# Relu² attention, Fourier mixing and a feed-forward block on one core: the last four token groups' first products taken jointly in two pairs, two first groups of 384 tokens, add and relu fused, and single events of the order model delayed or claimed

## The chip, the cores and the metric

One core of a Trainium2 chip runs the whole program. The metric is the device time of one execution in microseconds (us); for the kernel before, three runs gave 577.59, 578.49 and 578.52 us, median 578.49. Beside the times there is one profiled execution of it. Engines are named as the profile names them: PE multiplies matrices, PEld loads its weights, DVE, ACT and POOL work elementwise, SP issues most of the transfers. PSUM is the memory into which PE accumulates, SBUF the one that holds everything else on the core.

## What is computed

Eight batches, twelve heads, 448 positions, head size 64; the twelve heads side by side give rows of 768. The feed-forward block widens 768 to 3072 and back.

```python
scores = scale * np.matmul(q, k.transpose(0, 1, 3, 2))
attn = np.maximum(scores, 0.0) ** 2 / S
x = np.matmul(attn, v)                      # heads side by side: (8, 448, 768)
mixed = np.real(np.fft.fft(np.fft.fft(x, axis=1), axis=2))
u = x + mixed
un = (u - mean(u)) / np.sqrt(var(u) + 1e-06)
out = u + np.maximum(un @ w_ch1, 0.0) @ w_ch2
```

## The kernel before, in words

**Stages.** For each batch the program makes scores on PE (`score`), takes relu on ACT and the square on DVE or ACT (`squares`, `square`), multiplies by v (`attention`), folds the result and multiplies it by tables of cosines and sines (`fold`, `halves`, `mix`, `mix_rows`), adds x, normalises the rows (`rows` inside `mix_rows`), and stores u and the normalised un in DRAM (`u_store`, `n_store`). `turns` reads un back transposed, by transposing transfers that SP issues, into the tiles `unT`. The 3584 rows of all batches are then cut into token groups by the list `GT`, and `ffn` multiplies one group after another by the two weights. Groups do not end where batches do.

**Groups.** Before, `GT` gives groups of 384, 512 and 384 tokens and then nine of 256, numbered 0 to 11. A group's first product is 24 column blocks of w_ch1, each six matmuls with as many columns as the group has tokens (L1793); relu takes the sums out of PSUM into `hT`. The second product goes by blocks of 128 tokens. A block can be taken alone (`WHOLES`, `whole`), with 4 times 12 matmuls of 384 columns, or two blocks can be taken as a pair (`PAIRS`, class `Pair`), with 7 times 12 (L1933). The pair gets by with seven products in place of eight, as fast 2x2 block multiplication does, by using sums of blocks of `hT` (`Pair.early`, `Pair.late` on DVE) and sums of blocks of w_ch2 (`weight_sums`). What a product adds to the output goes through `add` (L1515) on DVE to a tile `o`, which holds rows of u and is then stored by SP (`outputs`).

**The last two groups.** Groups 10 and 11 take also the first product in that way (`last_two`): for each of twelve steps i, `main`, `second` and `third` issue seven products of three matmuls with 256 columns (L1635) in place of eight. Their operands are sums of blocks of w_ch1, made in SBUF that attention has left (`quarter_sums`, L1549, 24 sums of 768 columns), and four sums `Tk` of the two groups' `unT` (L1586). Partial sums are copied from PSUM by ACT (`copy`, L1644); DVE adds such a copy to another PSUM tile (`sum_out`, L1649) and takes the relu of the result in a second instruction (L1652). A `unT` tile has two homes that groups use in turn; a home is free when the group in it has ended its first product (`BUNT`).

**What sets the order.** Nothing is ordered by hand. Each stage is a generator that says which engine it needs, for how long by a model, and after what (`need`). `Streams.run` takes at each step the stream that could start earliest by the model and, between equals, the one of the lower rank, and emits it, so the order on every engine is fixed when the program is built. On the chip semaphores keep it correct, and an engine waits where the model was too hopeful. Attention on the later batches is let in between feed-forward matmuls by the rule `lead`: a piece of attention waits until `progress` (feed-forward work done, in batches) has come within `LEAD` of it.

## Time and profile before

| | us |
|---|---|
| three runs, median (lowest, highest) | 578.49 (577.59, 578.52) |
| span of the profiled execution, first to last instruction | 576.0 |
| median of the runs less that span | 2.5 |
| PE busy in it | 565.0 |
| DVE, ACT, POOL busy in it | 446.9, 336.9, 134.0 |

The page has no time of its own for the profiled execution beside its span; what lies around a span (launch and end) is taken as the 2.5 us by which the median of the runs exceeds it. Busy times are unions of an engine's instructions. A matmul's own duration in the profile runs from its start to its modelled end and overlaps with the next one's, so a rate is read from a run of many matmuls (length over count), not from the mean of one. Stretches are given in us from the span's start.

### The profile page before, as it was taken

How to read it: one execution, taken by the hardware profiler on the slowest of the kernel's cores; microseconds unless marked ns; L12 is line 12 of the kernel's file. 1: busy time of each engine (PE TensorE's matmuls, PEld its weight loads, DVE VectorE, ACT ScalarE, POOL GpSimd, SP SyncE). 2: the span in 40 equal slices, each digit the busy share in tenths (PEclk: the TensorE clock that was granted, in tenths of full speed). 3: DMA queues.
4: the chain of work that ended last, by engine and by line, in shares of the span. 5: the costliest groups of instructions: out<-in, count | busy, mean ns of one | idle time of the engine just before them, and what ended most of it. 6: DMA issues, size and time to landing. Idle time of an engine off the chain costs nothing.

```text
span 576.0 us, 11341 instructions
## 1 busy us (share of the span) xinstructions
PE 565.0 (98%) x4339; PEld 358.5 (62%) x4344; DVE 446.9 (78%) x1030; ACT 336.9 (59%) x538; POOL 134.0 (23%) x187
## 2 busy tenths in 40 slices
PE   8999999999999999999999999999999999999997
PEld 6466556544465546556757567568567786868864
DVE  6988775986688877997798879978978994267872
ACT  5977772977745676667559658856573160406400
POOL 8527102410134113321333116112220230000000
PEclk9999999999999999999999999999999999999999
DMA  9999999656938985799769977996654342223012
GB/s 125 206 211 249 202 219 181 174 109 78 202 78 223 175 140 119 161 167 193 140 136 197 201 126 161 177 173 113 141 107 94 109 142 85 66 73 93 2 41 97
DMA packets 133505, 81.84 MB, mean 142 GB/s; under 512 B 77516, under 2 KB 128716, under 8 KB 133452
## 3 DMA queue, kind: packets, MB, share of 16 engines
q0 software_dynamic: 40320, 33.63, 37.2%
q1 hardware_dynamic: 93132, 47.50, 36.6%
q8 instruction: 34, 0.56, 0.4%
q14 instruction: 19, 0.16, 0.1%
HBM read 62.91 MB, written 26.25 MB: 155 GB/s over the span
## 4 chain that ended last, share of the span: by engine, by line
PE 87%; DVE 9%; ACT 3%; issue 1%; DVEq 0%; ACTq 0%
PE psF L1793 31%; PE psF L1933 21%; PE psS L857 6%; PE psF L785 5%; PE psF L1821 4%; PE psS L1933 4%; PE psS L1635 3%; PE psF L1848 3%; PE psS L1332 2%; DVE sq L887 2%; ACT sq L870 1%; PE psS L785 1%; PE psS L2011 1%; PE psF L1635 1%; PE psS L932 1%; PE psS L1307 1%
## 5 line engine op out<-in xcount | busy, mean ns | idle before, releaser
L1793 PE MATMUL psF<-unT,w 128*128 128x256 bf16 (+2 forms) x1435 | 197.6, 294 | 1.3 <-ACT hT L1780 0.7
L870 ACT ACTIVATE sq<-psS 112x896 bf16<-112x896 f32 x192 | 165.2, 930 | 39.6 <-PE psS L857 39.2
L1793 PEld LDWEIGHTS <-w 128*128 128x128 bf16 x1440 | 137.5, 98 | 58.7 <-issue 12.9
L887 DVE TENSOR_TENSOR sq<-sq 112x896 bf16<-112x896 bf16 x163 | 98.4, 620 | 15.9 <-ACT sq L870 14.9
L1780 ACT ACTIVATE hT<-psF 128x512 bf16<-128x512 f32 (+3 forms) x144 | 71.7, 513 | 66.5 <-PE psF L1793 65.3
L1933 PEld LDWEIGHTS <-hT 128*128 128x128 bf16 x720 | 69.0, 98 | 50.3 <-issue 5.9
L1933 PE MATMUL psF<-w,hT 128*128 128x384 bf16 x378 | 67.1, 326 | 0.7 <-DVE xT L612 0.7
L1515 DVE TENSOR_TENSOR o<-psF,o 128x384 f32<-128x384 f32 x80 | 44.2, 553 | 25.2 <-PE psF L1933 20.8
L857 PE MATMUL psS<-qkT 64*128 64x448 bf16 (+1 forms) x384 | 52.8, 358 | 2.5 <-ACT sq L870 1.9
L413 POOL DMA_DIRECT2D vn<-in_v_dram x24 | 17.5, 730 | 105.4 <-PE psS L857 86.0
L1176 POOL TENSOR_TENSOR u<-tp,xn 112x385 f32<-112x385 f32 (+2 forms) x14 | 13.6, 974 | 109.0 <-DVE tp L1158 81.8
L857 PEld LDWEIGHTS <-qkT 64*128 64x128 bf16 (+1 forms) x384 | 17.3, 101 | 31.1 <-issue 24.1
L612 DVE TENSOR_SCALAR xT<-psF 128x224 bf16<-128x224 f32 x54 | 18.5, 383 | 21.8 <-PE psF L785 21.7
L785 PE MATMUL psF<-sq,vn 112*64 112x448 bf16 x264 | 31.3, 358 | 0.9 <-DVE hT L1778 0.9
L1204 ACT ACTIVATE un<-u,nmr,rstd 113x768 bf16<-113x768 f32 (+2 forms) x23 | 23.0, 1022 | 14.9 <-DVE nmr L1191 14.6
L413 POOL DMA_DIRECT2D qn<-in_q_dram x21 | 15.2, 724 | 62.7 <-DVE qkr L509 53.0
L1933 PE MATMUL psF<-wsum,hT 128*128 128x384 bf16 x162 | 28.8, 326 | 0.0
L1185 DVE BATCH_NORM_STATS2 stats<-u 112x6 f32<-112x384 f32 (+2 forms) x56 | 28.8, 540 | 0.0
L785 PEld LDWEIGHTS <-vn 112*64 112x64 bf16 x336 | 15.8, 109 | 19.6 <-issue 13.4
L884 ACT ACTIVATE sq<-sq 112x896 bf16<-112x896 bf16 x29 | 27.3, 950 | 0.5
L1821 PE MATMUL psF<-w,hT 128*128 128x384 bf16 x144 | 24.9, 326 | 0.0
L1848 PE MATMUL psF<-w,hT 128*128 128x384 bf16 x144 | 24.4, 326 | 0.0
(228 smaller groups left out, 783.2 us busy)
## 6 DMA issues: line engine op xcount, KB each, us to landing
out_dram<-o SPq DMA_DIRECT2D x56, 192.0 KB, 2.3
vn<-in_v_dram POOLq DMA_DIRECT2D x24, 224.0 KB, 5.0
qn<-in_q_dram POOLq DMA_DIRECT2D x21, 224.0 KB, 4.5
kn<-in_k_dram POOLq DMA_DIRECT2D x21, 224.0 KB, 7.3
w<-in_moe_w_ch_dram POOLq DMA_DIRECT2D x12, 384.0 KB, 13.2
w<-in_moe_w_ch_dram POOLq DMA_DIRECT2D x4, 1152.0 KB, 15.5
utop<-u SPq DMA_DIRECT2D x12, 336.0 KB, 3.8
o<-utop SPq DMA_DIRECT2D x16, 192.0 KB, 4.2
```

Of the source, the lines that this page charges most:

```text
L413: nc.gpsimd.dma_start(out=t, in_=src[b, hs].rearrange("h (p j) d -> p h (j d)", j=4))
L785: nc.tensor.matmul(av[h * Dh:(h + 1) * Dh, 0:S], lhsT=vn[:, c, h0 + h, :], rhs=sq[:, h, :], start=(c == 0), stop=(c == 3))
L857: nc.tensor.matmul(sc[:wide, h, 0:S].rearrange("k (c q) -> k c q", c=4), lhsT=flat[ps, k0:k0 + wide], rhs=qT[ps, m % 2], start=True, stop= ...
L870: nc.scalar.activation(r, sc[:R, :, 0:S], AF.Relu)
L887: nc.vector.tensor_tensor(r, r, r, op=ALU.mult)
L1185: nc.vector.bn_stats(stats[:n, hf, :], u[:n, hf * (D // 2):(hf + 1) * (D // 2)])
L1515: nc.vector.tensor_tensor(o, pc[:, 0:DH], o, op=ALU.add)
L1780: nc.scalar.activation(hs, ps, AF.Relu)
L1793: nc.tensor.matmul(ph[:, i * N:(i + 1) * N], lhsT=w1_sb[m][hf][:, (jj + i) * 128:(jj + i + 1) * 128], rhs=unT[:, m, 0:N], start=(m == 0), ...
L1821: nc.tensor.matmul(pc[:, 0:DH], lhsT=block(j, c), rhs=w2(j, hf), start=(j == 0), stop=(j == JC - 1))
L1848: nc.tensor.matmul(pc[:, 0:DH], lhsT=block(2 * i + k, c), rhs=weights[i], start=(start and i == 0), stop=(i == KP - 1), skip_group_check=True)
L1933: nc.tensor.matmul(pc[:, 0:DH], lhsT=lhs[i], rhs=rhs[i], start=(start and i == 0), stop=(i == KP - 1), skip_group_check=True)
```

## The change

Seven things change.

1. `GT` becomes 384, 384 and then eleven groups of 256; there are 13 groups, 0 to 12. `WHOLES` becomes `[[0, 1, 2], [2]]` and all groups but the first have one pair.
2. `last_two` becomes `joint(number)`, and runs twice: groups 9 and 10, then groups 11 and 12 (`JOINTS`). The buffers that the two share are taken once (`spread`), the four `Tk` are made once for each, and the `unT` homes of groups 9 and 10 are free when all 36 ends of their first products have been issued (`through`). The second group's block sums get tiles of their own (`ownsum`).
3. `sum_out` issues one instruction, `TENSOR_ADD_SAT` with the limits 0 and the largest float, for the add and the relu.
4. Of batch 1 the 128 rows of the second tile no longer are turned on PE; they go to DRAM by a new `part_store` (one scattering store by POOL, one row by SP) and come back by `turns`.
5. `HEAD` and `NUDGE` shift the model's start time of some kinds of events, or of single ones, when streams are compared; the start that is booked afterwards is the unshifted one.
6. The model's turned q and k count as ready 1.1055 us later (`TURNED`), stored rows 1.0 us later (`STORED`); `LEAD` is 2.7 less a slope of 0.1 for each batch still to come.
7. The fourth weight sum is made once and not partly twice; `Banks.take` may choose a PSUM bank by which tile its neighbour is in (`apart`).

```diff
@@ -57,9 +62,24 @@
+HEAD = {
+    ('attentions', 'PE', 2): -0.6, ('attentions', 'PE', 3): -0.619, ('chain_b', 'PE', 2): 0.232,
...
+}
+NUDGE = {
+    ('attentions.1', 45): 0.8, ('attentions.1', 48): 0.28, ('chain_a.1', 4): 0.28, ('chain_a.1', 8): 0.8,
...
+}
@@ -112,7 +138,7 @@
-                key = (ok is not None and not ok(), max(t), s[1][eng != "PE"])
+                key = (ok is not None and not ok(), max(t) + HEAD.get((s[3], eng, phase), 0.0) + NUDGE.get((s[4], s[5]), 0.0), s[1][eng != "PE"])
@@ -194,12 +222,13 @@
-    GT = [0, 384, 896] + list(range(1280, B * S + 1, 256))
+    GT = [0, 384] + list(range(768, B * S + 1, 256))
...
+    JOINTS = list(range(9, NGR, 2))
@@ -521,9 +551,9 @@
-                    c.t = e
+                    c.t = e + TURNED
@@ -749,7 +779,8 @@
-            lead = b + ((p if n else pa) - (0 if left is None else 4)) / NB - LEAD
+            lead = b + ((p if n else pa) - (0 if left is None else 4)) / NB
+            lead -= LEAD - SLOPE * (B - lead)
@@ -1259,6 +1291,19 @@
+    def part_store(ch, t):
+
+        un = lambda: uns[1][2 * ch + 1]
+        if ch:
+            e = yield need("SP", 0.1, [t])
+            nc.sync.dma_start(out=nbot[1][HS - 128:HS - 127, :], in_=un()[0:1])
+            n_stored[1][3].t = sch.dma(e, D * 2)
+            return
+        e = yield need("POOL", 1.1, [t])
+        nc.gpsimd.indirect_dma_start(out=nbot[1], out_offset=bass.IndirectOffsetOnAxis(ap=back[0], axis=0),
+                                     in_=un(), in_offset=None)
+        n_stored[1][1].t = sch.dma(e, 128 * D * 2) + 1.0
@@ -1379,7 +1430,7 @@
-    WHOLES = [[0, 1, 2], [2, 3], [2]] + [[]] * (NGR - 3)
+    WHOLES = [[0, 1, 2], [2]] + [[]] * (NGR - 2)
     PAIRS = [[], [0]] + [[0]] * (NGR - 2)
@@ -1498,10 +1550,11 @@
-        for b in range(NGR - 2):
+        for b in range(JOINTS[0]):
             yield need("SP", 0.0, [group_ready[b]])
             yield from ffn(b)
-        yield from last_two()
+        for n in range(len(JOINTS)):
+            yield from joint(n)
@@ -1577,20 +1636,20 @@
+        for c, g in enumerate(JOINTS):
+            yield need("DVE", 0.0, [group_ready[g], group_ready[g + 1]])
+            b1, b2 = groups[g][2], groups[g + 1][2]
...
@@ -1635,7 +1704,13 @@
+        def through(e):
+            to_go[0] -= 1
+            if not to_go[0]:
+                BUNT.free += [e, e]
@@ -1646,10 +1721,8 @@
             e = yield need("DVE", dve(N), deps, [BH[t]] if hta is not None else [])
-            nc.vector.tensor_tensor(dst, q[:, 0:N], u, op=ALU.add)
+            nc.vector._custom_dve(TENSOR_ADD_SAT, out=dst, in0=q[:, 0:N], in1=u, s0=FMAX, s1=0.0)
             done(e)
-            e = yield need("DVE", 0.2)
-            nc.vector.tensor_scalar(dst, dst, 0.0, None, op0=ALU.max)
             return e + LATENCY["DVE"] + SLACK
```

How the change moves instructions is shown at three places, with the numbers of the tiles. The first is DVE at the start of the joint stage; `hT` and `hB` are the relu'd first products of the two groups, `copies` the partial sums that ACT copied, `psS` and `psF` tiles of PSUM. Before:

```order
L1649 TENSOR_TENSOR hT_968<-psS_7062,copies_7065 128x256
L1652 TENSOR_SCALAR hT_968<-hT_968 128x256
L1649 TENSOR_TENSOR hT_968<-psS_7063,copies_7066 128x256
L1652 TENSOR_SCALAR hT_968<-hT_968 128x256
L1649 TENSOR_TENSOR hT_968<-psS_7064,copies_7067 128x256
```

And now:

```order
L1724 ISA hT_968<-psS_6621,copies_6624 128x256
L1724 ISA hT_968<-psS_6622,copies_6625 128x256
L1724 ISA hT_968<-psS_6623,copies_6626 128x256
L1724 ISA hT_968<-psF_6651,copies_6629 128x256
L1724 ISA hB_6513<-psS_6621,copies_6624 128x256
L1724 ISA hB_6513<-psS_6622,copies_6625 128x256
```

Each add with its relu has become one instruction, 36 for each joint, and no relu stands behind it on DVE.

The second place is SP's queue ahead of the program's last two groups: the transposing transfers that bring their `unT` from the stored rows (`ntop` and `nbot` with a batch's number), and what each waits for. Before (the transposes for group 11 stand twelve rows below those for group 10 that are shown):

```order
L1239 DMA ntop7_93<-un_6621 112x768 [waits DMAHW1_49,Activation_49]
L1280 DMA_TRANSPOSE unT_3354<-nbot6_100 128x6x64 [waits PE_49]
L1280 DMA_TRANSPOSE unT_3354<-ntop7_93 128x6x192 [waits DMAHW3_49,DMAHW1_49]
L1496 DMA out_0_dram<-o_6542 128x384 [waits DMAHW4_49,DVE_49]
L1496 DMA out_0_dram<-o_6559 128x384 [waits DMAHW5_49,DVE_49]
L1496 DMA out_0_dram<-o_6557 128x384 [waits DMAHW6_49,DVE_49]
```

And now, in front of groups 11 and 12:

```order
L1544 DMA o_6703<-ubot5_82 128x384 [waits DMAHW4_49]
L1324 DMA_TRANSPOSE unT_2455<-nbot6_100 128x6x64 [waits PE_49]
L1324 DMA_TRANSPOSE unT_2455<-ntop7_93 128x6x192 [waits DMAHW0_49]
L1324 DMA_TRANSPOSE unT_2455<-ntop7_93 128x6x32 [waits DMAHW1_49,PE_49]
L1548 DMA out_0_dram<-o_6632 128x384 [waits DMAHW2_49,DVE_49]
L1324 DMA_TRANSPOSE unT_2455<-nbot7_101 128x6x224 [waits DMAHW3_49,DMASW4_49]
```

The transposes of both groups now stand together behind a wait for PE, with the store of the output tile `o_6632` between them, which waits for DVE. On DVE the second and last add to that tile stands here, behind the sums of the first joint's pair (`s2` is a sum of blocks of `hT`):

```order
L1996 TENSOR_TENSOR hT_968<-hT_968,s2_2224 128x6x128
L1996 TENSOR_TENSOR hT_968<-hT_968 128x4x128
L1996 TENSOR_TENSOR hT_968<-hT_968 128x2x128
L1568 TENSOR_TENSOR o_6632<-psS_6622,o_6632 128x384
L1984 TENSOR_TENSOR quarter_6474<-hB_6516 128x256
```

So group 12 is asked for once that add is done.

The third place is DVE around the last batch's mixing (its `CAST pc`), where the sums of w_ch1 blocks (`quarter`) begin; `tp`, `qs` and `u` belong to the batch's rows. Before:

```order
L1515 TENSOR_TENSOR o_6128<-psF_6315,o_6128 128x384
L1158 TENSOR_TENSOR tp_6351<-psS_6332,qs_6348 113x385
L1160 TENSOR_TENSOR qs_6348<-psS_6332,qs_6348 113x385
L1549 TENSOR_TENSOR quarter_6306<-w1_4_0_502,quarter_6305 128x768
L1515 TENSOR_TENSOR o_6128<-psF_6217,o_6128 128x384
L1176 TENSOR_TENSOR u_6375<-qs_6348,xn_5833 113x385
L1178 TENSOR_TENSOR u_6375<-tp_6351,xn_5833 113x383
```

And now:

```order
L1402 CAST pc_6175<-psS_6145 114x2x2x193
L1603 TENSOR_TENSOR quarter_6105<-quarter_6104,w1_1_0_463 128x768
L1603 TENSOR_TENSOR quarter_6106<-w1_4_0_502,quarter_6105 128x768
L1568 TENSOR_TENSOR o_5933<-psF_6162,o_5933 128x384
L1603 TENSOR_TENSOR quarter_6107<-w1_2_0_483,w1_5_0_516 128x768
L1189 TENSOR_TENSOR tp_6198<-psS_6179,qs_6195 113x385
L1191 TENSOR_TENSOR qs_6195<-psS_6179,qs_6195 113x385
```

The sums stand among the last batch's rows as before, two more of them ahead of the rows; behind them one group's two products lie ahead of the joint stage, where there were two groups.

More of the change, by code (lines that the diff above doesn't have):

```diff
@@ L45, in __init__, with take @@
         self.make, self.ids, self.tiles = make, [(0.0, i) for i in range(n)], {}
-    def take(self):
+    def take(self, apart=None):
         first = min(self.ids)
+        if apart is not None:
+            held = {i // 2 for _, i in self.tiles.values() if i < 6}
+            first = min(self.ids, key=lambda x: (x[0] > apart, x[1] // 2 in held, x))
         self.ids.remove(first)
@@ L105, in run @@
             best = spare = None
+            now = self.engine["PE"]
+            phase = sum(now >= x for x in PHASES)
             for s in self.streams:
@@ L124, in run @@
                 best = spare
-            (_, start, _), s = best
+            s = best[1]
             eng, dur, deps, bufs, ok = s[2]
+            start = max([self.engine[eng]] + [d.t if isinstance(d, Cell) else d for d in deps]
+                        + [sorted(p.free)[bufs.count(p) - 1] for p in set(bufs)])
             for p in bufs:
@@ L1271, in turns @@
                 n = n_stored[bb]
-                deps = n[half::2]
+                yield need("SP", 0.0, n[half::2])
+                deps = [c.t + STORED for c in n[half::2]]
                 e = yield need("SP", 1.5, deps, [BUNT] if g is None else [])
-                if g is None and k == 2:
-                    g = work.tile([128, MC, 512], BF16, name="unT", tag="unT1", bufs=1)
-                elif g is None:
+                if g is None:
                     if pair_homes is None:
@@ L1286, in second_turned, with left @@
     def second_turned():
+        second_un[2].t = 0.0
         yield need("SP", 0.0, second_un)
-        e = max(c.t for c in second_un)
-        BUN[0].free.append(e)
-        un_left.t = group_ready[1].t = e
+        group_ready[1].t = max(c.t for c in second_un)
+        def left():
+            yield need("SP", 0.0, n_stored[1][1::2])
+            un_left.t = max(c.t for c in second_un + n_stored[1][1::2])
+            BUN[0].free.append(un_left.t)
+        sch.add(left(), (1, 1))
     first_pps, first_chan = [None, None], [Cell(), Cell()]
@@ L1567, in quarter_sums @@
                 yield from form(4, m, hf, w1_part(0, m + 3, hf), S_[2][m, hf], ALU.subtract)
-        ga, gb = NGR - 2, NGR - 1
+        yield need("DVE", 0.0, [], [BQ[0][1], BQ[1][1]])
+        for n, x in enumerate("qk"):
+            own[n].append((0, 8, work.tile([128, 8, 128], BF16, name="ownsum", tag=f"{x}n1", bufs=1)))
         yield need("DVE", 0.0, [un_ready[B - 1][1]], [BXN] + [BQ[2]] * 3)
@@ L1704, in third @@
             product(q, 1, 3, i, Tk[4], False, True)
+            through(e1)
             def leave(e):
@@ L1729, in last_two @@
             sch.add(p.chain_b(), (6.9 + 1 * n, 0))
-        yield need("SP", 0.0, pairs[1].done)
+        yield need("SP", 0.0, pairs[0].done + pairs[1].done)
+        for x in BH:
+            x.free.append(max(d.t for p in pairs for d in p.done))
     class Set:
```

134 lines of the change are left out of this document (77 added, 57 removed), and 5 rows, old and new, of the table NUDGE.

## The prediction

> **What bounds the kernel now.** I read the page's busy times and slices first, then busy times by stretch, then the chain of waits.
>
> ```profile
> span 576.0 us, 11341 instructions
> PE 565.0 (98%) x4339; PEld 358.5 (62%) x4344; DVE 446.9 (78%) x1030; ACT 336.9 (59%) x538; POOL 134.0 (23%) x187
> PE   8999999999999999999999999999999999999997
> DVE  6988775986688877997798879978978994267872
> PE 87%; DVE 9%; ACT 3%; issue 1%; DVEq 0%; ACTq 0%
> ```
>
> PE is full in all slices but the first and the last; DVE is the next engine. Where PE is not busy shows by stretch: 0 to 92 us (start), to 448 (attention mixed with the feed-forward block; at 448.13 the last batch is mixed), to 517 (two groups alone), to 550 (the joint first product), to the end.
>
> ```profile
> core 0: us, PE busy (x) PEld busy (x) DVE busy (x) ACT busy (x) POOL busy (x), PEclk, DMA share, GB/s
> 0.00:92.20 92.20, 86.75 (x804) 52.51 (x805) 70.82 (x168) 66.65 (x101) 40.61 (x83) 1.00 1.18 199
> ...
> 92.20:448.13 355.93, 353.94 (x2587) 213.36 (x2591) 292.81 (x647) 232.84 (x354) 84.47 (x96) 1.00 0.81 150
> 448.13:517.18 69.05, 69.05 (x533) 51.67 (x531) 44.92 (x100) 20.86 (x35) 8.90 (x8) 1.00 0.30 94
> 517.18:550.14 32.96, 32.80 (x285) 27.68 (x283) 26.80 (x85) 16.60 (x48) 0.00 (x0) 1.00 0.15 46
> 550.14:576.00 25.86, 22.43 (x139) 13.31 (x136) 11.52 (x31) 0.00 (x0) 0.00 (x0) 1.00 0.22 77
> ```
>
> PE is idle 5.45 us before 92 us, 1.99 in the long middle, 0.16 in the joint product and 3.43 at the end. The granted clock is 1.00 throughout. So the span is PE's work plus 11 us, and a change is worth what it takes from PE's work, unless something new makes PE wait.
>
> **The change, part by part.** PE's rates come from unbroken runs in the chain of waits (start, length, what, number of matmuls):
>
> ```profile
> 124.96 5.29 PE psF L1793 x24
> 136.46 3.99 PE psF L1793 x18
> 458.60 15.72 PE psF L1793 x144
> 474.32 13.66 PE psF L1933 x84
> 529.89 2.62 PE psS L1635 x24
> 570.62 1.96 PE psS L1933 x12
> 572.61 0.56 DVE o L1515
> ```
>
> A matmul of 512 columns (first two rows) costs 220 to 222 ns, one of 256 109.2 (15.72 / 144; 2.62 / 24 says the same of the joint product), one of 384 162.6 (13.66 / 84).
>
> *First products.* Counted over both programs, seven plain groups of 256 and two of 384 stay; what goes is the group of 512, 144 matmuls: 144 x 0.2204 = 31.7 us. What comes is a second joint, 12 x 7 x 3 = 252 matmuls: 252 x 0.1092 = 27.5 us. Net -4.2. Bounds: the rates of 256 and 384 lie on a line of 0.417 ns a column plus 2.4 ns, which makes 512 cost 216 ns, 31.1 us and a net of -3.6; the busy time of the 512 rows as it stands, 32.2 below, makes it -4.7.
>
> ```profile
> L1793 PE MATMUL psF<-unT,w 128*128 128x512 bf16 x139 | 32.2, 380 | 0.3
> L1108 PE MATMUL psS<-rev,un x18: 190/208/219, 48.0 to 114.1; 128*128 128x64 bf16 x6, 128*128 128x127 bf16 x6, 97*128 97x97 bf16 x6
> ```
>
> *Second products.* Six of the 28 blocks were taken alone and eleven pairs; now four and twelve. A pair has 84 matmuls, two single blocks 96: -12 x 0.1626 = -1.95.
>
> *Rows turned on PE.* Six matmuls of 127 columns go (second row above); at half of a 256-column one, 0.055 each, -0.33. In their place stand one scattering store on POOL, one row and two more transposes on SP. POOL's busiest stretch here is 40.6 of 92.2 us, and neither is on PE's path; I cost this at nothing. It would cost something if group 2 waited for those rows; group 2's first product stands behind group 1's two, which is 144 x 0.163 + 132 x 0.1626 = 45 us of cover.
>
> *Fused add and relu.* The nearest rows of DVE, the add and the relu:
>
> ```profile
> L1649 DVE TENSOR_TENSOR hT<-psS,copies 128x256 bf16<-128x256 f32 x16 | 6.7, 421 | 1.5 <-ACT copies L1644 1.3 <-PE psS L1635 0.2
> L1652 DVE TENSOR_SCALAR hT<-hT 128x256 bf16<-128x256 bf16 x24 | 5.4, 227 | 0.8
> ```
>
> The fused instruction costs at least the add, 0.42 us, and I take that, since it reads and writes the same tiles; the upper bound is both, 0.65. In either case PE, idle 0.16 us of the joint product, gains at most that. What hides it is PE itself. It turns into a loss only when DVE becomes the joint's bound: DVE is busy 26.80 of 32.96 us there, so 36 instructions may each be 0.17 us dearer than the two of today, 0.82 in all.
>
> *Second joint.* The first joint follows on the last plain group with 84 matmuls (13.7 us) for its setup, as today. The second one is new: its two `unT` can be fetched only when the first joint has ended its first products. The nearest rows are today's transposes (issue and landing) and what DVE then makes of them:
>
> ```profile
> 503.73 1.17 SPq L1280 DMA_TRANSPOSE unT<-ntop  x1
> 504.94 1.37 SPq L1280 DMA_TRANSPOSE unT<-nbot  x1
> DMA to landing us min/median/max: 2.3/4.1/6.8
> 510.06 0.55 DVE L1586 TENSOR_TENSOR chan<-unT 128x768 bf16<-128x768 bf16 x1
> 510.64 0.56 DVE L1586 TENSOR_TENSOR chan<-unT,chan 128x768 bf16<-128x768 bf16 x1
> ```
>
> Four transposes are 5 us of issue, the last lands within 6.8, and the second sum, the first that PE wants, is 1.1 later: 13 us. The store between them waits for an add on DVE behind three pair operations, some 2 to 3 us after the fetches begin. That makes 16 us, and it lies under 138 matmuls of the first joint's second product, 22.4 us. Cost nothing, with 6 us to spare; behind those transposes SP holds only loads and stores of `o` for the same stage.
>
> *Squeezed middle.* This is the part that speaks against the change. Of the feed-forward work one group of 256 (144 x 0.1092 + 84 x 0.1626 = 29.4 us of PE) no longer lies before the last batch's mixing; the attention and mixing work of all batches stays there. So the middle, 355.9 us, becomes 326.5. DVE loses there that group's adds and pair operations:
>
> ```profile
> L1515 DVE TENSOR_TENSOR o<-psF,o 128x384 f32<-128x384 f32 x80 | 44.2, 553 | 25.2 <-PE psF L1933 20.8 <-PE psF L1848 3.1 <-PE psF L1821 0.6
> L1911 DVE TENSOR_TENSOR s<-s,hT 128x768 bf16<-128x768 bf16 x10 | 6.1, 606 | 0.2
> L1911 DVE TENSOR_TENSOR hT<-hT 128x512 bf16<-128x512 bf16 x10 | 4.2, 425 | 0.3
> L1911 DVE TENSOR_TENSOR hT<-hT 128x256 bf16<-128x256 bf16 x10 | 2.9, 292 | 0.3
> ```
>
> Seven adds are 3.9 us; four operations of each of three widths, at these rows' price, 5.3. DVE's load goes from 292.8 / 355.9 = 82% to 283.6 / 326.5 = 87%. PE's stalls need not grow by that, since stretches denser than this exist today:
>
> ```profile
> 100.00:120.00 20.00, 19.98 (x145) 11.07 (x144) 19.36 (x49) 15.62 (x24) 6.85 (x8) 1.00 0.61 155
> 400.00:420.00 20.00, 19.89 (x142) 11.60 (x140) 19.25 (x49) 12.81 (x20) 4.83 (x5) 1.00 0.76 157
> ```
>
> DVE was 97% busy there and PE lost 0.02 and 0.11 us. ACT is far off (232.8 / 326.5 is still 71%).
>
> *Order model.* The shifts and later ready times can only move PE's idle time. PE's order is the same through the first 47.7 us, up to the first feed-forward matmuls, so the start cannot gain much. In the middle there are 1.99 us to be had, mostly in two single stalls:
>
> ```profile
> PE psF L785 <- DVE hT L1778: 0.9, 1, 0.9
> PE psF L1933 <- DVE xT L612: 0.7, 1, 0.7
> ```
>
> Bounds: -2.0 if all of it goes, +3 if each of the six batches' stretches gains a stall of 0.5, half of the longer one here. I take -0.5: the model now counts turned and stored rows as later, which removes too hopeful placements, against a denser DVE.
>
> **Sum.** -4.2 - 1.95 - 0.33 - 0.5 = -7.0; the span goes from 576.0 to 569.0. The median of the runs lies 2.5 us above the span, so 571.5 us.
>
> **The rivals.** *More idle time goes:* all 2 us of the middle and the dearest reading of the 512 group: -4.7 - 1.95 - 0.33 - 2.0 = -9.0, 569.5 us. For it: the edits are aimed at single events; against it: the middle gets denser.
>
> *The second joint starts late:* if the store between the transposes waits for the pair's later adds, 10 us more, the 16 us become 26 against 22.4, and PE stalls 3.6 us: 575.1. Against it: that add's product is among the first six matmuls of the 138.
>
> *DVE becomes the bound of the middle (the other side).* If the 82% that DVE had is all that its waits for other engines allow, the middle takes 283.6 / 0.823 = 344.6 us instead of 326.5, and the run 571.5 + 18.1 = 589.6 us. It decides from 283.6 / (326.5 + 7.0) = 85%: below that reachable load the kernel is slower, and just there the gain is given back and nothing changes. For it: DVE is 9% of the chain. Against it: the two 97% stretches.
>
> *Price per matmul, not per column.* If a stream of matmuls hid part of the longer ones, so that 512 columns cost no more than 384, the 144 that go would be worth 144 x 0.1626 = 23.4 us against 27.5 that come: +4.1 in place of -4.2, and 571.5 + 8.3 = 579.8 us. The rows above are against it: 220 for 512 against 162.6 and 109.2, in step with the columns. The Trainium skill (TensorE: Matmul & The Clock Gate, Back-to-back issue gap) goes further: in a real stream of load and multiply pairs about 131 ns for each 512-column matmul and 81 for one of 128. By it the 144 would be worth only 18.9 us, an estimate, and the change a loss; this trace is such a stream and does not agree with it.
>
> *The fused instruction is dear:* at 1.0 us, 0.18 above the bearable 0.82, two joints lose 72 x 0.18 = 13 us: 584.5.
>
> **How the numbers follow.** Forecast 0.62, more idle time gone 0.14, late second joint 0.13: faster 0.89. Gain given back exactly 0.03: same. DVE-bound middle 0.06, price per matmul 0.01, dear instruction 0.01: slower 0.08. A measurement of this kernel can tell about 0.2%, 1.2 us, from no change. The likeliest case gives 571.5. The range goes from 568.9, just below the case of more idle time gone, to 576.5, which takes in the late joint and the +3 of the order model (575.0), and leaves the slower cases out.
>
> **What would show it.** In the changed profile: no 128x512 form of the first product; joint matmuls at 109 ns and 504 of them; PE's busy time down by about 6.5 us; PE idle near 2 us in the middle; PE running on from the first joint's last second product into the second joint with no gap; the fused instruction near 0.42 us. The prediction is wrong if PE's idle time in the middle grows by more than 4 us, if a gap of several us stands before the second joint, or if the fused instruction is over 0.8 us.

## The result and the profile after

The changed kernel takes 575.65 us (median of 20 runs, lowest 573.36) where the kernel before takes 578.15 beside it: a ratio of 0.9957, 95% interval 0.9946 to 0.9968. It is faster by 2.5 us; 7.0 had been forecast. Ratios, and the counts of runs below, leave out runs more than 1.5% above the fastest of their kernel: here two, of 584.3 and 588.5 us, at a granted clock of 0.98 and 0.97; the longest, of the five moved copies below, took 641.0. The profiled execution took 574.73 us, with a span of 572.7; the 18 runs that count have a median span of 573.4, so it is one of the better ones.

The page of the kernel after, its span, busy times, slices and chain:

```profile
span 572.7 us, 11611 instructions
PE 559.8 (98%) x4434; PEld 366.5 (64%) x4434; DVE 446.3 (78%) x1030; ACT 341.7 (60%) x573; POOL 143.4 (25%) x193
PE   8999999899999999999999999999999999999997
DVE  6988773999797488998998789889899747544843
PE 83%; DVE 8%; DMA 4%; ACT 3%; issue 1%; POOL 1%; DVEq 0%; POOLq 0%; ACTq 0%
```

PE is still the bound. New in the chain are 4% of DMA; over half of that is one transposing transfer, issued at 87.5 us and landed 12.4 us later. Busy times by stretch, cut at the same events as before (start, last batch's mixing at 418.54, the group behind it, the first joint, its second product, the second joint, the end):

```profile
core 0: us, PE busy (x) PEld busy (x) DVE busy (x) ACT busy (x) POOL busy (x), PEclk, DMA share, GB/s
0.00:92.20 92.20, 86.61 (x811) 52.16 (x812) 70.73 (x167) 67.15 (x102) 39.79 (x83) 1.00 1.18 199
92.20:418.54 326.34, 322.82 (x2484) 202.92 (x2483) 277.95 (x624) 228.84 (x353) 93.96 (x101) 1.00 0.86 157
418.54:458.37 39.83, 39.83 (x306) 29.51 (x305) 34.95 (x78) 12.56 (x22) 9.62 (x9) 1.00 0.47 131
458.37:489.00 30.63, 30.59 (x264) 25.64 (x263) 18.92 (x50) 15.84 (x46) 0.00 (x0) 1.00 0.22 58
489.00:514.00 25.00, 25.00 (x161) 15.47 (x159) 13.27 (x34) 0.73 (x2) 0.00 (x0) 1.00 0.29 90
514.00:547.00 33.00, 33.00 (x286) 27.74 (x284) 21.21 (x59) 16.52 (x48) 0.00 (x0) 1.00 0.15 44
547.00:572.70 25.70, 22.00 (x136) 13.02 (x133) 9.31 (x22) 0.00 (x0) 0.00 (x0) 0.99 0.22 77
```

Both joints run full, with no gap ahead of the second. The middle is 326.3 us, as worked out, but PE is idle 3.52 us in it where it was 1.99. Its waits there, with what ended each (us in total, times, longest), after:

```profile
PE psS L888 <- DVE qs L1191: 1.9, 2, 1.2
PE psF L816 <- DVE sq L918: 1.0, 2, 0.9
PE psF L1870 <- DVE xT L642: 0.2, 1, 0.2
```

The two waits of before, 0.9 and 0.7 us, are gone; 1.9 at 101 us and 1.0 at 246 us have come. For an account of the whole, each span is cut at the first feed-forward matmul, at the first matmul of the last mixing and at PE's end, and the feed-forward matmuls of a piece, counted in the program, are taken out at fixed rates (0.217, 0.1628 and 0.109 us for 512, 384 and 256 columns; the median distances between starts in these two traces are 216, 163 and 109 ns, and with 216 the second row below would read -5.60 and the third +1.79):

| us | before | after | change | forecast |
|---|---|---|---|---|
| up to the first feed-forward matmul | 51.66 | 51.31 | -0.35 | 0 |
| all feed-forward matmuls at these rates | 412.79 | 407.05 | -5.74 | -6.15 |
| from there to the last mixing, less these ("the middle's other time") | 104.90 | 106.83 | +1.93 | -0.83 |
| from the last mixing to PE's end, less these | 3.22 | 3.80 | +0.58 | 0 |
| PE's end to the span's end | 3.39 | 3.70 | +0.31 | 0 |
| span | 575.96 | 572.69 | -3.27 | -7.0 |

The work went as forecast to within 0.4 to 0.6 us. What is missing beside that is 2.8 us in the middle and 0.9 behind it; 1.5 of the 1.9 us in the middle are the added idle time of PE. The middle's other time is used below to compare profiles.

### The profile page after: what moved, and what is told of

It is laid out like the page before. It is cut to its first block, busy times and chain, and to the rows that moved or that the text cites. A ratio compares the mean times of both kernels' runs of the same rounds, so it can differ in the third digit from the quotient of the medians.

```text
span 572.7 us, 11611 instructions
## 1 busy us (share of the span) xinstructions
PE 559.8 (98%) x4434; PEld 366.5 (64%) x4434; DVE 446.3 (78%) x1030; ACT 341.7 (60%) x573; POOL 143.4 (25%) x193
## 4 chain that ended last, share of the span: by engine, by line
PE 83%; DVE 8%; DMA 4%; ACT 3%; issue 1%; POOL 1%; DVEq 0%; POOLq 0%; ACTq 0%
PE psF L1870 24%; PE psF L2008 22%; PE psS L1704 7%; PE psS L2008 7%; PE psS L888 6%; PE psF L816 4%; PE psF L1898 3%; PE psF L1704 2%; DMA qkT<-qkr 2%; PE psS L1383 2%; ACT sq L901 2%; DVE sq L918 2%; DMA qk<-in_k_dram 2%; PE psF L1923 1%; PE psS L816 1%
## 5 line engine op out<-in xcount | busy, mean ns | idle before, releaser
L1870 PE MATMUL psF<-unT,w 128*128 128x256 bf16 (+1 forms) x1296 | 165.8, 285 | 1.0 <-ACT hT L1857 0.7
L1870 PEld LDWEIGHTS <-w 128*128 128x128 bf16 x1296 | 123.6, 98 | 42.4 <-issue 10.8
L1857 ACT ACTIVATE hT<-psF 128x512 bf16<-128x512 f32 (+3 forms) x136 | 66.2, 504 | 37.9 <-PE psF L1870 37.1
L2008 PE MATMUL psF<-w,hT 128*128 128x384 bf16 x378 | 67.1, 326 | 0.0
L1568 DVE TENSOR_TENSOR o<-psF,o 128x384 f32<-128x384 f32 x72 | 39.7, 551 | 14.3 <-PE psF L2008 12.6
L1719 ACT COPY copies<-psS 128x256 f32<-128x256 f32 x51 | 17.8, 374 | 29.0 <-PE psS L1704 26.3
L1704 PEld LDWEIGHTS <-w 128*128 128x128 bf16 x288 | 28.1, 98 | 4.3 <-issue 0.2
L915 ACT ACTIVATE sq<-sq 112x896 bf16<-112x896 bf16 x32 | 30.1, 955 | 0.3
L816 PEld LDWEIGHTS <-vn 112*64 112x64 bf16 x336 | 15.7, 109 | 19.1 <-issue 12.6
L1568 DVE TENSOR_TENSOR o<-psS,o 128x384 f32<-128x384 f32 x21 | 11.6, 556 | 20.2 <-PE psS L2008 20.2
## 6 DMA issues: line engine op xcount, KB each, us to landing
w<-in_moe_w_ch_dram POOLq DMA_DIRECT2D x12, 384.0 KB, 13.5
```

The source lines that it names most:

```text
L816: nc.tensor.matmul(av[h * Dh:(h + 1) * Dh, 0:S], lhsT=vn[:, c, h0 + h, :], rhs=sq[:, h, :], start=(c == 0), stop=(c == 3))
L915: nc.scalar.activation(r, r, AF.Square)
L1568: nc.vector.tensor_tensor(o, pc[:, 0:DH], o, op=ALU.add)
L1704: nc.tensor.matmul(ps[:, 0:N], lhsT=lhs, rhs=rhs[:, m], start=(start and m == 0), stop=(stop and m == 2), skip_group_check=True)
L1857: nc.scalar.activation(hs, ps, AF.Relu)
L1870: nc.tensor.matmul(ph[:, i * N:(i + 1) * N], lhsT=w1_sb[m][hf][:, (jj + i) * 128:(jj + i + 1) * 128], rhs=unT[:, m, 0:N], start=(m == 0), ...
```

## The experiments

Theory A: the work's gain came in full, and a denser middle with a late DVE gave part back. B: the shifts of single events cause the new waits. C: the shifts are needed, and without them the new groups fit worse. D: the wait at 101 us hangs on a transfer's time and differs between executions of one order.

**The order model taken back.** Four kernels keep groups, joints, stores and the fused instruction, and change only the tables:

```diff
-HEAD = {...}                  (13 entries)
-NUDGE = {...}                 (24 entries)
+HEAD, NUDGE = {}, {}                                        # no shifts
+TURNED = STORED = 0.0; LEAD = 2.6; SPARE = 0.5; SLOPE = 0.0  # besides, for the model of before
+HEAD = {('attentions', 'PE', 2): -0.6, ('attentions', 'PE', 3): -0.619}   # attention's two alone
+NUDGE = {}                                                  # HEAD whole
```

> The changed kernel with HEAD and NUDGE empty; groups, joints, fused instruction and the changed model times stay. Theory A (the 6.5 us less of PE work came in full, and about 3 us were given back to new waits, because the middle stretch has become denser and DVE is late there): what the empty tables do is let feed-forward work back between the attention, so that the last batch's mixing comes just ahead of the first joint (48 matmuls between them, where there were 228 and more). The waits of the middle shrink to 2 us or less, but the first joint starts without cover for its sums and waits 2 to 6 us: 575 to 579 us. Theory B (the shifts of single events themselves cause the new waits): without them PE idles 2 us in the middle and nothing is added at the joint: 572 to 573 us. Theory C (the shifts are worth what they were put there for, and the middle without them is worse): PE idles 5 us or more in the middle, 578 us and more.

> As the kernel without HEAD and NUDGE, and with the model's times of before (TURNED and STORED 0, LEAD 2.6, SLOPE 0): the groups, the two joints and the fused instruction under the old order rules. Theory A: PE's order is nearly that of the kernel without shifts, the middle idles about 2 us as in the kernel before, and the start of the joint costs 2 to 6 us: 575 to 579 us. Theory B: 572 to 573 us. If the later ready times matter, it is 1 us or more slower than the kernel without shifts alone, by waits for turned q and k or stored rows.

> The changed kernel with only two of the shifts, those that claim attention on PE 0.6 us early in two phases; the other eleven of HEAD and all of NUDGE are left out. Without any shift it took 607 us, with 13.5 us lost where group 2 waits for its transposed rows, 10.7 us and more where the first joint waits for its sums, and 4 us of slower clock behind the first. If these two entries alone are what puts group 8 behind the last mixing (84 second-product and 12 first-product matmuls then stand between the two, by the order) and batch 2's rows ahead of group 2, both waits go and the time is 576 to 581 us. If the single-event shifts carry it, it stays above 590 us.

> The changed kernel with HEAD whole and NUDGE empty. With neither it took 607 us, with two entries of HEAD 601 us. By the order, 228 feed-forward matmuls and more stand between the last mixing and the first joint here, as in the changed kernel. If HEAD carries the gain, 576 to 580 us, and the single events of NUDGE are worth 0 to 4 us. If NUDGE carries what keeps group 2's rows on time, a wait of 10 us and more stands ahead of group 2 and the time is 588 us or above.

| kernel | us | ratio to before (interval) |
|---|---|---|
| no shifts | 607.0 | 1.0506 (1.0489 to 1.0524) |
| no shifts, model of before | 611.2 | 1.0576 (1.0557 to 1.0595) |
| attention's two shifts alone | 601.0 | 1.0387 (1.0350 to 1.0425) |
| HEAD whole, no NUDGE | 597.8 | 1.0332 (1.0313 to 1.0350) |

No theory had foreseen such sizes; C has the sign, and B is out. The model's changed times and `LEAD` are worth something too: without them 4 us more are lost. PE's longest waits in the kernel without shifts:

```profile
PE psF L1870 <- DMA unT<-ntop: 13.5, 1, 13.5
PE psS L1704 <- DVE hT L1724: 11.5, 3, 10.7
PE psF L1870 <- DVE xT L642: 2.1, 2, 1.5
```

Group 2's first product waits for its transposed rows, and the first joint for the sums of w_ch1 blocks: with only 36 second-product matmuls between the last batch's rows and the joint (the expectation counted a step too early), where the changed kernel has 228, DVE still makes the rows' statistics and these sums when PE arrives. In the changed kernel neither wait exists, since its order brings attention forward, and with it batch 2's rows, and keeps a whole group for the time behind the mixing. With attention's two shifts alone the waits are 11.5 and 5.9 us; with HEAD whole the one for group 2's rows is 3.7 and a new one of 7.5 us stands at 275 us, for an output add on DVE. So HEAD does not carry it alone: it takes 9 us off 607, and NUDGE on top of it 22 off what is left. NUDGE without HEAD was not run, nor shifts of its own for the kernel before. The long wait also costs clock; the stretches around it:

```profile
180.00:195.80 15.80, 2.36 (x17) 1.09 (x15) 8.86 (x20) 5.72 (x8) 7.98 (x9) 0.72 0.83 179
195.80:200.00 4.20, 4.19 (x20) 2.11 (x19) 0.00 (x0) 0.60 (x1) 0.00 (x0) 0.50 0.32 59
200.00:204.00 4.00, 4.00 (x37) 3.01 (x35) 3.37 (x8) 3.24 (x5) 0.00 (x0) 0.94 0.41 89
```

After 13.5 us of idleness PE ran its next 4.2 us at half clock and did 20 matmuls in them, where the next 4 us did 37. The Trainium skill (TensorE: Matmul & The Clock Gate, The HAM clock gate) says that the array falls to half its clock after an idle window of about 3.4 us and comes back after as long a busy one; the trace agrees.

**The number of joints.**

```diff
-    JOINTS = list(range(9, NGR, 2))
+    JOINTS = [11]            # one joint
+    JOINTS = [7, 9, 11]      # three joints
```

> The changed kernel with one joint (JOINTS = [11]); groups 9 and 10 take their products plainly, and PE's order is the same up to the start of the first joint. This measures the second joint's worth by itself: 288 plain matmuls of 256 columns in place of 252, so 36 x 0.109 = 3.9 us more work. If the joint costs what its matmuls cost, the run is 575.65 + 3.9 = 579.6 us (span 576.6). If the joints bring costs of their own (switching, waits for copies), it is less than 3 us above the changed kernel. The waits of the middle stay as they are in the changed kernel, 3.5 us before the last mixing, in either theory.

> The changed kernel with three joints (JOINTS = [7, 9, 11]): 3.9 us less of PE work again, but groups 7 and 8 no longer lie between the last batch's attention, so the middle is squeezed once more by one group's 29 us and the last three pieces of attention and the mixing run without any feed-forward work between them. Theory A (cover is what the squeeze uses up): PE idles 8 to 20 us more around the last mixing, 580 to 590 us. If the cover is not needed, 575.65 - 3.9 = 571.7 us.

One joint: 1.0019 of before (1.0001 to 1.0037), 0.0062 above the changed kernel, 3.6 us. That is the 3.9 us of its 36 matmuls within the width of the two intervals; a cost of its own of more than some 1.5 us is not there. This profile has the changed kernel's order up to the joint, and its wait at 101 us is not there; the middle's other time is 105.23. Three joints: 1.0849 (1.0808 to 1.0890), some 626 us. PE's waits:

```profile
PE psS L1704 <- DVE chan L1647: 11.6, 1, 11.6
PE psF L816 <- DVE sq L918: 11.4, 7, 9.3
PE psS L1704 <- DVE qs L1191: 5.5, 2, 4.3
PE psS L1383 <- DVE fold L733: 4.6, 1, 4.6
```

580 to 590 us had been expected. The waits stand at the last attention (9.3 us at 412), the mixing and the setup of the joint, which no longer have feed-forward work beside them: not one such matmul lies between 401 us and the first joint at 432. The tables of shifts were those for two joints, so how much of it three joints would lose with an order laid out for them is not shown.

**The same order again, and single instructions moved.** For these kernels the model's choices were recorded and played back, so that every instruction but those named keeps its place. First the changed order and the kernel before, once more each; then, on DVE alone, rows moved as follows:

```diff
 L539 COPY qkr<-qn                        rows first, at 100 us
-L539 COPY qkr<-kn
 L1189, L1191 tp, qs (four sums of batch 1's rows)
+L539 COPY qkr<-kn
 L715 folds<-xT                           squares first, at 244 us
+L918 sq<-sq x2
 L723 fold<-folds x2
-L918 sq<-sq x2
```

> The changed kernel once more, with the same order on every engine (the order is taken from a recorded list of the model's choices in place of the model itself; no instruction moves). It tells what differs from one execution to the next. Theory D (the 1.9 us of PE waits at 101.5 us, where scores wait for a PSUM tile that batch 1's rows still hold, come from a transposing transfer that lands late in some executions; the profile of the kernel with one joint has the same order there and does not show them): this profile may or may not show them, its span then is 572.7 or about 571; the median of its runs is 574.7 to 576.5. If instead they belong to the order, they stand here again with 1.2 + 0.7 us.

> The kernel before, unchanged, profiled a second time. If the transfers' timing is what moves the middle, and its slack hides it there, the middle (first feed-forward matmul to last mixing, less the feed-forward work in it) is again 104.9 us within 0.3 us and DVE waits some 5 us for transposing transfers, with no PE wait of over 1 us behind 92 us. If it comes out 1 to 2 us longer, the kernel before has the same changes from execution to execution, and the loss of 1.9 us in the changed kernel's profile is not the change's.

> The changed kernel's order once more. Four profiles of DVE's order at 101 us have shown the waits of 1.9 to 2.6 us there in two and not in the other two. Expected: a span of 571.3 to 574 us, the middle 105.2 to 105.5 us without a wait over 1 us, or 106.8 to 107.7 with one; median of the runs 574.5 to 576 us.

> The same recorded order with one instruction moved: on DVE the copy of batch 3's k (qkr<-kn, L539), which waited 4.4 us for a transposing transfer, goes behind the four sums of batch 1's rows (L1189, L1191), for which the scores on PE wait. Theory D: the 1.9 us at 101.5 us can no longer occur, since those sums need no transfer; the median falls by 1 to 2 us against the changed kernel, 574 to 575 us, and the spread of the runs gets narrower. If the wait's cost is taken back by the next wait (the turned k comes later), nothing is gained: 575.6.

> The same recorded order with two squares (L918) moved ahead of two fold sums (L723, 1.48 us together) on DVE, at 244.5 us, where PE waited 0.88 + 0.16 us for the squares in three profiles of this order. If PE's wait there is a matter of this place in DVE's queue alone, it falls to nothing and the time by 0.9 us: about 574.7 us. If DVE is simply behind there, by its load, the wait comes back later in the same stretch (220 to 300 us) and nothing is gained: 575.6.

> Both moves together. If the two waits are all that the order lost in the middle, they add: 575.65 - 1.0 to 1.9 - 0.9 = 573 to 573.8 us, the best of these kernels. If one frees only what the other then loses, it equals the better of the two.

> The changed order with the copy of k behind batch 1's rows and the two squares ahead of the fold sums, once more. If the two moves gain what the first look said, the fast runs have a median of 573.5 to 574.5 us, 0.9925 of the kernel before. If that was chance between executions, 575 to 576 us, as the changed order.

| kernel | ratio to before (interval) | middle's other time | PE's wait at 101 us |
|---|---|---|---|
| before; before again | 1; one profile alone | 104.90; 105.13 | 0; 0 |
| changed; same order; order again | 0.9957 (0.9946 to 0.9968); 0.9935 (0.9905 to 0.9966); 0.9918 (0.9899 to 0.9937) | 106.83; 107.66; 106.09 | 1.9; 2.6; 1.3 |
| rows first | 0.9925 (0.9900 to 0.9950) | 106.16 | 0 |
| squares first | 0.9954 (0.9934 to 0.9975) | 105.47 | 0 |
| both; both again | 0.9926 (0.9897 to 0.9955); 0.9926 (0.9900 to 0.9952) | 106.28; 105.95 | 0; 0 |

Theory D holds: the wait comes with 1.3 to 2.6 us or not at all, in one and the same order (squares first has this place unchanged too; 0.7 of the 2.6 is PE's own wait for the turned k). Where it comes, DVE shows why. Its timeline in the changed kernel (start, length, what, in brackets the idle time ahead and what ended it):

```profile
100.00 0.43 DVE L539 COPY qkr<-kn 112x1024 bf16<-112x1024 bf16 x1 [4.37 <-DMA qkT<-qkr]
100.34 0.55 DVE L1189 TENSOR_TENSOR tp<-psS,qs 128x385 f32<-128x385 f32 x1
100.92 0.56 DVE L1191 TENSOR_TENSOR qs<-psS,qs 128x385 f32<-128x385 f32 x1
```

The copy of k has one buffer and waits until the transfer that transposes the k before has read it; batch 1's rows stand behind the copy, their PSUM tile stays held, and the scores on PE wait for it. In the profile with one joint the same copy:

```profile
97.92 0.43 DVE L539 COPY qkr<-kn 112x1024 bf16<-112x1024 bf16 x1 [1.19 <-DMA qkT<-qkr]
98.26 0.55 DVE L1189 TENSOR_TENSOR tp<-psS,qs 128x385 f32<-128x385 f32 x1
```

In that stretch the DMA engines are full. The transfer that reads the k before is issued at 87 to 90 us, and the profiles of this place line up by how long it holds the buffer (from its issue to the start of the copy):

| profile | transfer, us | DVE stands, us | PE waits for the rows, us |
|---|---|---|---|
| changed; same order; order again | 12.5; 12.6; 11.7 | 4.4; 4.5; 3.6 | 1.9; 1.9; 1.3 |
| one joint; squares first; unfused (below) | 9.3; 9.3; 9.7 | 1.2; 1.1; 1.6 | 0; 0; 0 |
| rows first; both; both again | 12.2; 12.0; 11.9 | 0.6; 0.4; 0.3 | 0; 0; 0 |

Moved behind the rows, the copy no longer holds them up, and the wait at 101 us is gone in all three profiles with that move, though the transfer was late in each. All three have 0.7 + 0.4 us at 208 to 212 us instead, for `xT` and then an output add behind the next such copy, on which DVE stood 3.0 to 3.1 us. Of the six profiles without the move only that of the unfused kernel has this, so it can come without the move; whether the move makes it likelier is not shown. The squares ahead of the folds take most of the 1.0 us at 246 us away, and 0.6 to 1.3 us come at 248 to 263, as that run's other reading had it: DVE is behind there by its load, busy 18.24 of the 20 us from 240 to 260 with both moves. Over 18 runs both moves give a median of 574.3 us, the changed order over its 26 (three sets) 574.9; the intervals overlap, and whether the 0.6 us are real stays open.

**More copies moved.** The same was tried at each place where DVE stood behind such a copy: at 100, 207, 257, 301 and 318 us, one to four instructions back (one square goes from DVE to ACT by it); the same with the squares; and the four without that at 318 us, with the squares.

> The recorded order of the changed kernel with five copies of k (qkr<-kn, L539) moved one to four places back on DVE, at 100, 207, 257, 301 and 318 us, where DVE stood 1 to 4.4 us behind such a copy until a transposing transfer had read the buffer (11.2 us of DVE in the changed kernel's profile, 4.8 us in that of the kernel before). One square falls to ACT instead of DVE. Theory D+ (in the denser middle DVE has no slack, and what it loses behind these transfers comes back as PE waits): DVE's waits for the transfers fall to 4 us or less, PE's waits at 101 and 208 us go, and the median is 573 to 574.5 us. Rival: PE needs those turned keys as early as they come, and the waits only move to the scores: 575 to 576.5 us.

> The same five moves and the two squares of the earlier run ahead of the fold sums at 244.5 us. If DVE, less late now, can take the squares early and the folds in time, the 1.0 us at 246 us goes for good: 1 us below the run with the copies alone, 572 to 573.5 us. If DVE is behind there by its load, it comes back at 248 to 263 us as it did before (0.6 + 0.3 + 0.4 us) and the two kernels are equal.

> The recorded order with the copies of k at 100, 207, 257 and 301 us later and the two squares at 244.5 us earlier, but the copy at 318 us left in its place (moved back it brought a wait of 0.8 to 2.2 us at 321). If the waits are places in DVE's queue that can each be ordered away, the middle falls to 104.5 to 105 us, and the median to 573 to 574 us, 1.5 to 2 us below the changed order on the same chip. If the denser middle loses about the same wherever the queue is mended, the middle stays at 105.2 us or more and the median within 1 us of it.

Ratios 0.9953 (0.9928 to 0.9977), 0.9971 (0.9945 to 0.9997) and 1.0007 (0.9980 to 1.0034): no gain, and with four moves the change's whole gain is lost. The first two of these kernels did cut DVE's waits for the transfers, to 5.7 and 4.6 us from 10.7, and yet the middle's other time is 107.4 and 105.5 us (111.3 with four moves): D+ fails, and the waits move, as its rival had it. All three profiles have a new wait of PE at 320 to 323 us (2.2, 0.8 and 4.3 us), which none of the nine others of this order has; in the first two it is a wait for the transposing transfer itself. With four moves, the longest waits of PE and of DVE in the middle:

```profile
PE psS L888 <- DVE pc L1402: 4.3, 1, 4.3
```

```profile
DVE qkr L539 <- DMA qkT<-qkr: 10.4, 4, 7.7
```

DVE stood 7.7 us at the copy of k at 322 us, with a cast of the mixing behind it, and PE waited for the cast. The transposing transfer that held the buffer was issued at 315.2 us, as in the changed kernel (315.4), but the copy followed 6.6 us later and not 3.1. In the two others it followed after 6.7 and 5.4 us, and in all three an issue at 305 to 306 us held SP for 4.6 to 4.8 us, longer than any in the other profiles. Why the moves make the transfer land late is not settled; that the wait comes with them is shown by three profiles against nine. The wait with four moves also cost clock, and PE did 17 matmuls in the 3.8 us behind it:

```profile
318.90:323.20 4.30, 0.05 (x2) 0.10 (x1) 1.41 (x3) 1.62 (x2) 0.69 (x1) 0.79 0.89 147
323.20:327.00 3.80, 3.80 (x17) 2.47 (x17) 2.53 (x6) 0.92 (x1) 0.01 (x1) 0.50 1.04 188
```

Behind the 2.2 us with five moves the granted clock stayed at 1.00.

**The fused instruction.** In the recorded order each fused instruction is made two again; and in the kernel before it is put in, all else in place:

```diff
-            nc.vector._custom_dve(TENSOR_ADD_SAT, out=dst, in0=q[:, 0:N], in1=u, s0=FMAX, s1=0.0)
+            nc.vector.tensor_tensor(dst, q[:, 0:N], u, op=ALU.add)
+            nc.vector.tensor_scalar(dst, dst, 0.0, None, op0=ALU.max)
```

> The recorded order of the changed kernel with each fused add and relu of the joints again as two DVE instructions, 72 relus more at about 0.23 us, 16 us of DVE in the two joint first products (21.2 of 33 us busy in the second). If the fusing is hidden under PE, as costed, nothing changes: 575.2 to 576 us. If DVE's queue sets when PSUM comes free there, PE waits: up to 2 x 36 x 0.23 = 16 us at the worst, 577 us and more if a fifth of it shows.

> The kernel before with add and relu of its one joint fused (36 relus fewer on DVE), the order of every engine otherwise the same. As costed, PE was idle 0.16 us in that joint, so at most that is gained: 577.9 to 578.4 us, no difference. If the relus also hold PE up where the profile of before does not show it (the joint of the changed order lost 3.2 us for its 72 without being the dearer by the profile's bound), 1 to 1.6 us are gained: 576.5 to 577 us.

Unfused, the changed order takes 0.9994 of before (0.9972 to 1.0015), 0.4% more than with the fused one: without this instruction the rest of the change cannot be told from no change. Its profile loses 6.98 us from the last mixing to PE's end, less the feed-forward matmuls, where the changed kernel loses 3.80. PE's waits in the joints, none of which the changed kernel has:

```profile
PE psS L1704 <- DVE hT L1724: 1.3, 4, 0.5
PE psS L1704 <- DVE hB L1724: 0.5, 1, 0.5
PE psS L1704 <- ACT hB L1748: 0.3, 1, 0.3
```

In the kernel before the fused one gives 0.9974 (0.9950 to 0.9999), 1.5 us with an interval from almost nothing to 2.9, between the two cases expected; in its profile the same stretch goes from 3.22 to 2.91 us, and what the rest would be is open. So by the ratios the larger part of the 0.9957 may be this one instruction's. That profile also shows that the kernel before is not free of the wait at 101 us: 0.7 us there, 105.83 us of other time in the middle. With it the kernel before has 104.9 to 105.8 in three profiles, mean 105.3, and the changed order 105.2 to 107.7 in five (those of the table, of one joint and of the unfused order, 106.27), mean 106.4.

## Why the prediction was right in its direction and wrong in its size

**What bounds the kernel:** right. PE is full, at a clock of 1.00, and the change is worth what it takes from PE's work, less new waits. None of the three signs of being wrong came (idle time in the middle up by 4 us, a gap ahead of the second joint, a fused instruction over 0.8 us); they were too coarse for what went wrong. The time lies inside the range, near its slow end, because that end took in 3 us of new stalls.

**First products, -4.2:** right to 0.6. The 512-column matmuls cost 216 ns (their median distance) and not 220.4, which came from one stretch of 24, so 31.1 us went and 27.5 came: -3.6, the bound that the prediction had drawn from the rates of 256 and 384 columns. The joints' rows are at 109 ns a matmul (start, length, what, number):

```profile
458.37 2.29 PE psS L1704 x21
```

The rival of a price per matmul falls with it. The 131 ns of the Trainium skill (TensorE: Matmul & The Clock Gate, Back-to-back issue gap) do not hold here either. The formula of the Trainium skill for a single matmul in the same place, columns / 2.4 + 2.5 ns, gives 215.8, 162.5 and 109.2, within 0.5 ns of the medians in these traces.

**Second products, -1.95:** right; twelve matmuls of 163 ns. **Rows turned on PE, -0.33:** six matmuls fewer, too small to be told apart.

**Fused instruction, 0:** its duration was right, 0.42 us (the medians of its four forms are 418 to 425 ns; the largest group):

```profile
L1724 DVE CUSTOM_DVE_ANT_0 hT<-psS,copies x39: 414/424/426, 459.5 to 544.8; 128x256 bf16<-128x256 f32 x39
```

For the one joint of before it gains 0.3 us by the profile and 1.5 by the runs, barely clear of nothing. So the bound, "PE gains at most the 0.16 us idle", does not hold for certain even there, and in the new order two joints without it lose 3.2 us in the profile: it is a condition of the gain. That order was laid out for the fused instruction; one laid out for two might lose less, which was not tried.

**Second joint's start, 0:** right; PE was busy 25.00 of the 25 us ahead of it, and the rival of a late start falls.

**Squeezed middle, 0, and order model, -0.5:** here the prediction failed. It took the shifts as trimming of 2 us of idle time, with +3 as the worst, and took the cover for group 2's rows and for the first joint's sums from the changed order as if the groups gave it. The runs show that the groups alone lose some 29 us against the kernel before and 31 against the changed one, and that the shifts give all of that back; what remains is +1.9 us of other time in the profiled execution, +1.1 between the means of five profiles and three, against the -0.83 of the sum. "Stretches denser than this exist today", DVE 97% busy and PE nearly full, was right as far as it went: DVE was busy 277.95 of 326.34 us, 85% (283.6 had been counted), and did not become the bound. What the load did not tell is what DVE waits for. It stood for transposing transfers 10.7 us in the middle, where it had stood 4.8 in the kernel before (7.5 to 11.1 in the five profiles of the changed order, 3.8 to 5.9 in the three of before), and it had 48.4 us idle there in all (326.34 - 277.95) where it had had 63.1. Before, and after:

```profile
DVE qkr L509 <- DMA qkT<-qkr: 4.8, 3, 2.2
DVE qkr L539 <- DMA qkT<-qkr: 10.7, 6, 4.4
```

So A is right in that the work came and the middle took part back, and D names the mechanism of the largest wait. That the density itself makes the transfers' time count is argued from these waits and not shown: two kernels with moved copies had DVE wait less for transfers and were no faster, and one with a second buffer for the copies was not run. So the failed step is known, the -0.5 for the order and the nothing for the squeeze; of its cause only the wait at 101 us is shown.

**Not in the sum:** 0.6 us between the last mixing and PE's end and 0.3 behind PE's last matmul. Every profile with two fused joints in this order has them (3.80 to 3.82 and 3.70 to 3.71, against 3.22 and 3.39); their cause was not looked for. The median of all 20 runs lies 0.9 us above the profiled execution. By the median span of the 18 runs that count, 573.4 against the 576.0 of the profile of before, the change is -2.6 and not -3.3, close to the -2.5 of the times; the 18 spread from 573.4 to 578.7, those of the kernel before from 577.1 to 578.6.

## What to carry to other kernels

When a change moves work between stages and also retunes the order, price the move under the old order as well: what the retuning had to repair here, some 30 us, was far more than the 2 us of idle time that the old profile showed. Cover that is counted in matmuls holds only as long as the order keeps those matmuls there. And before crediting a denser stretch, list what the second engine waits for: an instruction that waits for a transfer at the head of its queue turns the transfer's scatter into waits of the engine that bounds. Moving that instruction back took away the wait at one place here, with no gain in time that could be told from chance, and moving four or five brought a wait elsewhere. And take several profiles of one order before a wait is put down to it.

## What was not expected of the hardware

Transposing transfers scatter widely at one place of one order: the one at 87 to 90 us held its buffer for 9.3 to 12.6 us, with the DMA engines full, and with the copy ahead of the rows PE then waited 0 to 1.9 us for them. Issuing one kept SP 1.25 us in the median, over 1.5 us in 12 to 23 of the 98 or 100 of a profile, and 4.6 to 4.8 us once in each kernel with four or five moved copies. And waits of 13.5 and of 4.3 us were dearer than their length, by a granted clock of 0.50 in the 4.2 and 3.8 us behind them; behind the 1.9 us at 101 us and the 2.2 us at 322 the clock stayed at 1.00.
